# Block-sparse attention and Fourier mixing on one core: another order of the last output products and stores, and the first pair's k load cut in two

## The chip, the cores and the metric

The kernel runs as one program on one core of a Trainium2 chip. The core has a matrix engine (TensorE, "PE" in the profile; its weight loads are listed apart as "PEld"), a vector engine (VectorE, "DVE"), an activation engine (ScalarE, "ACT"), a general engine (GpSimd, "POOL") and a queue engine (SyncE, "SP"). SP and ACT both issue transfers here; the profile calls SP's transfer queue q1 and ACT's q10, and writes "SPq" and "ACTq" for the time in which the two issue them. All transfers run on the core's 16 DMA engines. The metric is the device time of one execution in microseconds (us), the median over several runs.

## The reference

Four batches, eight heads, 768 positions, head width 64. Attention is masked by blocks of 32: a block sees its neighbours, the first and the last block, and three sampled blocks.

```python
scores = scale * np.matmul(q, k.transpose(0, 1, 3, 2))
scores = np.where(mask, scores, -1000000000.0)
attn = softmax(scores)                       # over the last axis
x = np.matmul(attn, v)                       # then (B, H, S, D) -> (B, S, H*D)
u = x + np.real(fft(fft(x, axis=1), axis=2))
un = (u - mean(u)) / sqrt(var(u) + 1e-6)     # over the 512 channels
out = u + np.maximum(un @ w_ch1, 0.0) @ w_ch2    # 512 -> 2048 -> 512
```

## The kernel before, in words

**Attention.** Two heads of one batch make a pair; there are 16 pairs, and a pair goes through 12 units of one score product each (128 keys by 2 x 384 queries). `load_q` and `load_k` fetch a pair's rows, `turn` transposes them on PE and copies them to SBUF, `scores` (L569) multiplies, `weigh` takes the exponential on ACT (L589), `values` multiplies with v (L642). For the first pairs the mask is added by a second, small matmul (L579). A function `slot` runs two units at a time and puts other work between them by estimated times (`when`, `busy`, `gap`); what it plans is fixed when the program is built, and the order of the instructions on each engine is the order in which the code records them.

**The start.** The first pair's loads are recorded first: `load_k(0, nc.scalar)` puts both heads of k on ACT's queue (two transfers, 768 packets of 256 bytes each), `load_q(0)` puts q in six parts on SP's queue (three thirds `t` of the positions times two heads, 256 packets each). ACT then issues v of that pair. SP goes on with a weight chunk (`w_load`), the six parts of the next pair's q, another chunk, the next pair's k, and so on. On PE six matmuls of the unit matrix keep the engine busy (`warm`, L309); then `turn(0, 1, 0)` transposes the first half of k (three of its six chunks of 128 positions), `turn(0, 0, 0)` the first four of six parts of q (that is `t` = 0 and 1), seven more unit matmuls follow, and then come the first scores. The second half of k is transposed after the first two units, and `t` = 2 of q in slot 1. Every transfer counts on one of eight semaphores in turn, so that each one also waits until the transfer eight before it has landed.

**The weights.** w_ch1 and w_ch2 come in chunks of 512 KB and are split into the form that the matmuls want by ACT (L456, L459) and DVE during the first pairs.

**Mixing and channel mixing.** After a batch's attention, `mixer` computes the Fourier sums, the normalised rows, and the two channel products. For the last batch, which has nothing else to run beside it, both products use seven multiplications in place of eight (Winograd's form of Strassen's scheme): `quad` for the first product (seven products of 1.29 us each) and `outputs(r, m, after)` for the second. `outputs` is called for two halves r of the 2048 channels and, in each, for three blocks m of 128 rows; its code names four quarters of such a block's result: `a0` and `a1`, the left and right 256 columns of 128 rows in the first half of the positions (tile xA), and `b0` and `b1`, the same for 128 rows of the second half (xB). Each of its seven products is four matmuls of 128 x 256 into one PSUM buffer: two buffers "m", two "s", one "t" and one "o". `plus` adds a product to its quarter on DVE (L1166). The seven in the order before:

1. a11 with a block of w_ch2 (PSUM "m"): into u by an ACT copy (L1175), and into a0
2. a12 (PSUM "m"): into a0, which is then complete
3. a21 with right sum 2 (PSUM "t"): into u; then u into a1
4. left sum 1 with right sum 1, called `p5` (PSUM "o"): into a1 and, later, into b1
5. left sum 3 with right sum 3 (PSUM "s"): into u; then u into both halves of xB at once (L1188)
6. left sum 4, called `p3` (PSUM "m"): into a1, which is then complete
7. a22 with right sum 4 (PSUM "s"): into b0, which is then complete

Between them `ahead(j)` lets DVE compute the four left sums of the next block of rows (`output_left`, L1142), for m = 0 and 1; the sums 1 to 4 have to be made in that order, since sum 2 is written over a21.

**The stores.** In the second half (r = 1) `store(half, m, cols, queue)` (L1104 to L1107) writes 128 rows of the output. Because of the symmetry that the Fourier part uses, the rows of a block lie in the output in runs that `_ORDER` lists, and `_rows` makes them into transfers: block 0 and block 2 of the first half are two transfers of 64 rows each; block 1 has four, of 1, 63, 63 and 1 rows; in the second half block 3 (m = 0) and block 5 (m = 2) are one transfer of two runs of 64 rows, written "2x64" below, and block 4 (m = 1) is three, of 1, 2x63 and 1 rows. For the very last block of rows (`ends`: r = 1 and no next block) `store(1, m)` is cut by columns: 256 columns (b1) after step 5, and b0 in two parts of 128 columns at the end, one on SP's queue and one on ACT's.

**The exit.** After the last block the code has a branch over a second program (`general`, for inputs with very large scores; L1574). Each engine takes that branch when its own list ends; SP then waits for the eight transfer semaphores, and the engines meet in a last barrier.

Of the kernel before, what the change touches and what calls it, by code (L numbers as in the profile page):

```python
# [22 lines left out]
def _words(ap, n):  # L23

    return bass.DRamTensorHandle(ap.tensor.name, (2 * n,), I32)
# [57 lines left out]
def _rows(view, tile):  # L83

    got = []
    for t, p0, runs, jump, n, s0, step in _ORDER:
        if t != tile:
            continue
        at = view[s0:s0 + 1, :]
        row, col = list(at.ap[0])[0], list(at.ap[1])  # L90
        if jump > 0:
            got.append((p0, runs * n, bass.AP(tensor=at.tensor, offset=at.offset,
                                              ap=[[jump * row, runs], [step * row, n], col])))
            continue
        for r in range(runs):
            at = view[s0 + r * jump:s0 + r * jump + 1, :]
            got.append((p0 + r * n, n, bass.AP(tensor=at.tensor, offset=at.offset,
                                               ap=[[step * row, n], col])))
    return got
# [3 lines left out]
def kernel(  # L103
# [14 lines left out]
    nc = tc.nc  # L118

    B, H, S, D = q.shape  # L120
    DM = H * D
    FF = w_ch1.shape[1]
    P = 128
    C = S // P
# [8 lines left out]
    T = C // 2  # L133
# [48 lines left out]
    ps_s = ctx.enter_context(tc.tile_pool(name="ps_s", bufs=2, space=PSUM))  # L182
    ps_o = ctx.enter_context(tc.tile_pool(name="ps_o", bufs=1, space=PSUM))
# [5 lines left out]
    when = {"PE": 0.0, "ACT": 0.0, "DVE": 0.0, "POOL": 0.0}  # L189
    free = {"m": [0.0, 0.0], "t": [0.0]}  # L190

    def busy(engine, us, after=0.0):
        when[engine] = max(when[engine], after) + us
        return when[engine]
# [23 lines left out]
    def load_blocks(n, a, tile):  # L218


        b, j = pairs[n]
        for i in range(2):
            rows = (q, k)[a][b, 2 * j + i].rearrange("(t r) (g d) -> g r t d", r=BLK, d=BLK)
            for g in range(D // BLK):
                p0 = D * i + BLK * g
                nc.sync.dma_start(
                    out=tile[p0:p0 + BLK, :].rearrange("r (t d) -> r t d", d=BLK), in_=rows[g])
        loaded[n, a] = tile

    def load_k(n, queue=None):  # L230

        if n >= BY_VECTOR:
            load_blocks(n, 1, ld.tile([P, S], FP32, tag="k", name="kb"))
            return
        b, j = pairs[n]
        kt = loaded.get((n, 1))
        if kt is None:
            kt = ld.tile([P, C, 2, D], FP32, tag="k", name="kr")
        for i in range(2):
            (queue or nc.sync).dma_start(out=kt[:, :, i, :],  # L240
                                         in_=k[b, 2 * j + i].rearrange("(p c) d -> p c d", p=P))
        loaded[n, 1] = kt

    def load_q(n):

        if n >= BY_VECTOR:
            load_blocks(n, 0, ld.tile([P, S], FP32, tag="q", name="qb"))
            return
        b, j = pairs[n]
        qt = loaded.get((n, 0))  # L250
        if qt is None:
            qt = loaded[n, 0] = ld.tile([P, T, 2, 2, D], FP32, tag="q", name="qr")
        for t in range(T):
            for i in range(2):
                rows = q[b, 2 * j + i][2 * P * t:2 * P * (t + 1), :]
                nc.sync.dma_start(out=qt[:, t, :, i, :],
                                  in_=rows.rearrange("(p r) d -> p r d", r=2))
# [36 lines left out]
    def bit(n):  # L294
# [4 lines left out]
    nc.gpsimd.dma_start(out=samp_i.rearrange("a b c -> a (b c)"),  # L299
                      in_=bass.AP(tensor=_words(sampled_blocks, NB * NR), offset=0,  # L300
                                  ap=[[0, NB], [1, 2 * NB * NR]]))
    load_k(0, nc.scalar)
    load_q(0)

    def warm(n):

# [171 lines left out]
    by_pe, to_gather = set(), deque()  # L478
    masks = {"by_pe": True}
# [68 lines left out]
    UP = 2 * C  # L548
    UNITS = len(pairs) * UP
    SLOT = 2  # L550
# [59 lines left out]
    def gather(u):  # L610


        n, w = divmod(u, UP)
        half, c = divmod(w, C)
        if c == 0:
            return
        if c == 1:
            acc_of[n, half] = acc_p.tile([P, 2, HS], FP32, tag="acc", name="acc")
        acc, e = acc_of[n, half], e_of[u]
        start = e_of[u - 1] if c == 1 else acc  # L620
        at = max(e_at[u], acc_at.get((n, half), 0.0))
        if u in by_pe and masks["by_pe"] and w < UP - SLOT and max(when["DVE"], at) + 1.0 < max(when["POOL"], at) + 2.9:
            nc.vector.tensor_tensor(out=acc, in0=start, in1=e, op=ALU.add)
            acc_at[n, half] = busy("DVE", 1.0, at) + HOP
        else:

            for i in range(2):
                nc.gpsimd.tensor_add(out=acc[:, i, :], in0=start[:, i, :], in1=e[:, i, :])  # L628
            acc_at[n, half] = busy("POOL", 2.9, at) + HOP
        e_free[u] = acc_at[n, half]  # L630
# [320 lines left out]
    def mixer(b, xA, xB):  # L951
# [24 lines left out]
        t, s = {}, {}  # L976
# [127 lines left out]
        def store(half, m, cols=slice(0, DM), queue=nc.sync):  # L1104
            x = (xA, xB)[half]
            for p0, cnt, rows in _rows(out[b][:, cols], T * half + m):
                queue.dma_start(out=rows, in_=x[p0:p0 + cnt, m, cols])  # L1107
            if m == T - 1:
                finished.add((b, half))
# [5 lines left out]
        o_t, o_s = {}, {}  # L1115
        DH = DM // 2

        def block(r, k, n):
            return w2_sb[:, 8 * r + 4 * k:8 * r + 4 * k + 4, n * DH:n * DH + DH]
# [25 lines left out]
        def outputs(r, m, after):  # L1145

            if m == 0:
                output_left(m, 1)
                output_left(m, 2)
            a11, a12, a21, a22 = (hs[g, i][:, :, m * P:(m + 1) * P]  # L1150
                                  for i in range(2) for g in range(2))
            a0, a1 = xA[:, m, 0:DH], xA[:, m, DH:DM]
            b0, b1 = xB[:, m, 0:DH], xB[:, m, DH:DM]
            rights = {j: [o_t[j, 0], o_t[j, 1]] for j in (1, 2, 3, 4)}

            def product(pool, tag, a, c):
                ps = pool.tile([P, 512], FP32, tag=tag, name="yy")[:, 0:DH]
                for k in range(4):
                    nc.tensor.matmul(ps, a[:, k, :],  # L1159
                                     c[k // 2][:, k % 2, :] if isinstance(c, list) else c[:, k, :],  # L1160
                                     start=(k == 0), stop=(k == 3))
                busy("PE", 1.75)
                return ps

            def plus(to, a, c=None):
                tt(out=to, in0=a, in1=to if c is None else c, op=ALU.add)  # L1166
                busy("DVE", 0.43)

            def ahead(j):
                if after is not None:  # L1170
                    output_left(after, j)

            u = sum_p.tile([P, DH], FP32, tag="oT", name="u")
            p1 = product(ps_m, "m", a11, block(r, 0, 0))
            nc.scalar.copy(out=u, in_=p1)  # L1175
            plus(a0, p1)
            plus(a0, product(ps_m, "m", a12, block(r, 1, 0)))
            if m == 0:
                output_left(m, 3)
                output_left(m, 4)  # L1180
            plus(u, product(ps_t, "t", a21, rights[2]), u)
            plus(a1, u)
            p5 = product(ps_o, "o", o_s[m, 1], rights[1])
            plus(a1, p5)
            ahead(1)
            plus(u, product(ps_s, "s", o_s[m, 3], rights[3]), u)
            both = xB[:, m, :].rearrange("p (n d) -> p n d", n=2)
            tt(out=both, in0=both,  # L1188
               in1=u.rearrange("p (o d) -> p o d", o=1).broadcast_to([P, 2, DH]), op=ALU.add)
            busy("DVE", 0.7)  # L1190
            plus(b1, p5)
            ends = r == 1 and after is None
            if ends:
                store(1, m, slice(DH, DM))
            ahead(2)
            p3 = product(ps_m, "m", o_s[m, 4], block(r, 1, 1))
            plus(a1, p3)
            if r == 1:
                store(0, m)
            ahead(3)  # L1200
            ahead(4)
            plus(b0, product(ps_s, "s", a22, rights[4]))
            if ends:
                store(1, m, slice(0, P))
                store(1, m, slice(P, DH), nc.scalar)
            elif r == 1:
                store(1, m)

        fl = [[("tm"[h == 1 and m != 1], lambda h=h, m=m: un_flip(h, m), 0.6, 0.55, 0.0)
               for m in range(T)]  # L1210
# [6 lines left out]
              for m, us in (((0, 2), RIGHT), ((1,), COMBINE))]  # L1217
        le = [("d", lambda i=i: left(0, i), 0.0, 0.0, COMBINE) for i in (1, 3, 4)]
        after = ([fl[0][0], sp[1][0]] + le +
                 [fl[0][2], sp[1][2], wh[1][0], fl[0][1], sp[1][1], wh[1][2],  # L1220
                  fl[1][0], fl[1][2], wh[1][1]] + ri[0] + [fl[1][1]] + ri[1])
# [391 lines left out]
```

## Time and profile before

| what | value |
|---|---|
| median of 7 runs | 1065.64 us (1064.47 to 1066.08) |
| the profiled execution's own time | 1064.72 us |
| its span, first to last instruction | 1063.0 us |
| PE busy | 1037.4 us, 98% of the span |
| DVE, ACT, POOL busy | 62%, 35%, 22% |
| mean granted TensorE clock | 0.995 |
| PE idle in the last of 40 slices (1036.4 to 1063.0 us) | about half |
| PE waiting for q at the start | 0.4 us, once |

The profiled execution is longer than its span by 1.72 us, which lies outside the first and the last instruction. All times below are from the span's start. "Idle before, releaser" in a row says how long the engine stood still before it and what ended that; a row with "x8" merges eight instructions of one kind. PE's rows are pipelined, so their durations overlap a little; the chain of waits, which cuts them at their starts, is the better clock for PE.

### The profile page before, as it was taken

The numbers are of one execution on the slowest core, as the hardware profiler recorded it, in microseconds if no ns is written. First come the engines' busy times: TensorE is split into PE (matmuls) and PEld (weight loads), VectorE is DVE, ScalarE is ACT, GpSimd is POOL, SyncE is SP. The second block draws the span as 40 slices with busy tenths as digits, with TensorE's granted clock in tenths as the row PEclk, the third lists the DMA queues.
The fourth block names the chain that finished last, engine by engine and source line by source line (L and its number), as shares of the span: only waits on it lengthen the run. The fifth ranks groups of instructions, "written<-read, shape, count | busy, mean of one in ns | idle before, by whom it ended". The sixth has DMA issues, their size and how long they took to land.

```text
span 1063.0 us, 12409 instructions
## 1 busy us (share of the span) xinstructions
PE 1037.4 (98%) x4390; PEld 536.1 (50%) x4390; DVE 654.2 (62%) x1218; ACT 374.5 (35%) x742; POOL 235.7 (22%) x262
## 2 busy tenths in 40 slices
PE   8999999999999999999999999999999999999995
PEld 4433345444455554444444555444445554578584
DVE  5898995667645445664678364765457355574663
ACT  6978755664030112342441302353221211210210
POOL 1000183537000002454553001256420001000000
PEclk9999999999999999999999999999999999999998
DMA  7757422220000002212230001221000001000001
GB/s 209 225 177 226 121 46 45 45 47 15 1 0 1 1 0 48 59 31 52 42 55 1 1 0 30 60 38 28 11 12 5 1 0 34 27 0 1 1 20 43
DMA packets 120741, 46.65 MB, mean 44 GB/s; under 512 B 108114, under 2 KB 113632, under 8 KB 120672
## 3 DMA queue, kind: packets, MB, share of 16 engines
q1 hardware_dynamic: 118654, 44.92, 16.9%
q10 hardware_dynamic: 1986, 0.85, 0.3%
q8 instruction: 36, 0.59, 0.2%
q14 instruction: 33, 0.27, 0.1%
q0 software_dynamic: 32, 0.01, 0.0%
HBM read 37.11 MB, written 6.29 MB: 41 GB/s over the span
## 4 chain that ended last, share of the span: by engine, by line
PE 90%; ACT 3%; DVE 2%; DMA 2%; issue 1%; SPq 0%; POOL 0%; ACTq 0%; DVEq 0%
PE y L1096 23%; PE z L1040 15%; PE s L569 13%; PE o L642 11%; PE yp L1040 7%; PE yy L1159 7%; PE xp L1040 4%; PE zp L850 2%; PE s L579 1%; PE sp L709 1%; DMA out_dram<-x 1%; PE zp L822 1%; PE sp L723 1%; PE utp L965 1%; PE xt L665 1%
## 5 line engine op out<-in xcount | busy, mean ns | idle before, releaser
L628 POOL TENSOR_TENSOR acc<-acc,e 128x384 f32<-128x384 f32 x158 | 159.4, 1044 | 94.0 <-DVE e L599 75.0
L569 PE MATMUL s<-qT,kT 64*128 64x384 f32 x768 | 153.6, 515 | 7.5 <-ACT e L589 4.0
L642 PE MATMUL o<-e,vr 128*64 128x384 f32 x768 | 142.3, 498 | 0.0
L1096 PE MATMUL y<-w_sb,hB 128*128 128x512 f32 x288 | 128.2, 596 | 1.0 <-DVE x L1099 1.0
L1096 PE MATMUL y<-w_sb,hA 128*128 128x512 f32 x288 | 128.4, 595 | 0.0
L599 DVE TENSOR_TENSOR e<-s,mask 128x768 f32<-128x768 f32 x92 | 83.8, 950 | 57.8 <-ACT s L597 48.0
L1099 DVE TENSOR_TENSOR x<-y,x 128x512 f32<-128x512 f32 x72 | 49.7, 690 | 110.9 <-PE y L1096 110.8
L569 PEld LDWEIGHTS s<-qT,kT 64*128 64x128 f32 x768 | 63.9, 185 | 85.6 <-issue 21.9
L597 ACT ACTIVATE s<-s 128x768 f32<-128x768 f32 x92 | 69.9, 792 | 87.5 <-PE s L569 87.0
L1040 PE MATMUL z<-unT,t 128*128 128x384 f32 x256 | 93.1, 486 | 1.2 <-DVE hA L1045 1.2
L628 POOL TENSOR_TENSOR acc<-e 128x384 f32<-128x384 f32 x42 | 47.1, 1143 | 212.6 <-ACT e L589 127.6
L1045 DVE TENSOR_TENSOR hA<-z,hA 128x384 f32<-128x384 f32 x64 | 35.7, 557 | 87.3 <-PE z L1040 87.3
L589 ACT ACTIVATE e<-s 128x768 f32<-128x768 f32 x100 | 76.2, 816 | 36.7 <-PE s L579 31.6
L1096 PEld LDWEIGHTS y<-w_sb,hB 128*128 128x128 f32 x288 | 53.4, 190 | 67.7 <-issue 64.8
L913 POOL TENSOR_SCALAR st<-st 128x1 f32<-128x1 f32 x24 | 8.6, 359 | 346.9 <-DVE st L912 346.8
L1096 PEld LDWEIGHTS y<-w_sb,hA 128*128 128x128 f32 x288 | 53.3, 190 | 62.8 <-issue 59.7
L642 PEld LDWEIGHTS o<-e,vr 128*64 128x64 f32 x768 | 48.1, 137 | 70.6 <-issue 68.2
L1049 ACT ACTIVATE hA<-hA 128x384 f32<-128x384 f32 x64 | 33.5, 523 | 120.3 <-DVE hA L1045 119.8
L1040 PEld LDWEIGHTS z<-unT,t 128*128 128x128 f32 x256 | 48.5, 190 | 35.5 <-DVE hA L1045 2.1
L1049 ACT ACTIVATE hB<-hB 128x384 f32<-128x384 f32 x64 | 33.5, 523 | 86.5 <-DVE hB L1045 84.1
L1060 ACT COPY hA<-xp 128x384 f32<-128x384 f32 x32 | 15.3, 479 | 97.9 <-PE xp L1040 97.9
L1040 PE MATMUL xp<-unT,w_sb 128*128 128x384 f32 x128 | 47.3, 492 | 0.0
(202 smaller groups left out, 1431.3 us busy)
## 6 DMA issues: line engine op xcount, KB each, us to landing
wraw<-in_moe_w_ch_dram SPq DMA_DIRECT2D x32, 512.0 KB
vr<-in_v_dram SPq DMA_DIRECT2D x30, 192.0 KB
qb<-in_q_dram SPq DMA_DIRECT2D x44, 96.0 KB
kb<-in_k_dram SPq DMA_DIRECT2D x44, 96.0 KB
x<-oT SPq DMA_DIRECT2D x192, 12.0 KB
out_dram<-x SPq DMA_DIRECT2D x17, 128.0 KB
out_dram<-x SPq DMA_DIRECT2D x7, 256.0 KB
qr<-in_q_dram SPq DMA_DIRECT2D x24, 64.0 KB
```

Of the source, the lines that this page charges most:

```text
L569: nc.tensor.matmul(s[:, i, 0:HS], kT[rows, c * P:(c + 1) * P], qT[rows, queries], start=True, stop=u not in by_pe)
L589: nc.scalar.activation(out=e, in_=s[:, :, 0:HS], func=ACT.Exp, scale=scale)
L597: nc.scalar.activation(out=s[:, :, 0:HS], in_=s[:, :, 0:HS], func=ACT.Exp, scale=scale)
L599: nc.vector.tensor_tensor(out=e, in0=s[:, :, 0:HS], in1=m.broadcast_to([P, 2, HS]), op=ALU.mult)
L628: nc.gpsimd.tensor_add(out=acc[:, i, :], in0=start[:, i, :], in1=e[:, i, :])
L642: nc.tensor.matmul(o[D * i:D * i + D, :], vt[:, i, c, :], e[:, i, :], start=(c == 0), stop=(c == C - 1))
L1040: nc.tensor.matmul(to, a[:, k, :], c[:, k, :], start=(k == 0), stop=(k == ND // 2 - 1))
L1045: tt(out=to, in0=ps, in1=a, op=ALU.add)
L1049: nc.scalar.activation(out=h, in_=h, func=ACT.Relu)
L1096: nc.tensor.matmul(y, hs[0, half][:, l, m * P:(m + 1) * P], w2_sb[:, 4 * r + l, :], start=(l == 0), stop=(l == 3))
L1099: nc.vector.tensor_tensor(out=x[:, m, :], in0=y, in1=x[:, m, :], op=ALU.add)
L1159: nc.tensor.matmul(ps, a[:, k, :], c[k // 2][:, k % 2, :] if isinstance(c, list) else c[:, k, :], start=(k == 0), stop=(k == 3))
```

## The change

It has two parts.

**The first pair's loads.** `load_k` takes a list of cuts over the chunks and `load_q` a list of thirds. ACT's queue now gets only the first three of k's six chunks (two transfers of 384 packets); SP's queue gets the thirds 0 and 1 of q (four transfers), then the other three chunks of k (two transfers), then third 2 of q (two transfers). SP issues eight transfers there in place of six.

**The last outputs.** In `outputs`, for both r, product 7 of the list above (a22, into b0) moves to the fourth place, p5 from the fourth place to the sixth, and p3 becomes the last. The sum of p5 into b1 now stands ahead of its sum into a1. `ahead(1)`, `ahead(2)` and `ahead(3)` all come after these, ahead of p3's sum into a1; `ahead(4)` comes after it. With r = 1, block m of xB is stored before block m of xA. For the last block of rows, a0 is stored as soon as it is complete (two transfers of 64 rows x 256 columns on SP's queue), b0 after the sum of step 5 (2x64 rows x 256 columns, one transfer on ACT's queue), b1 after p5 (the same size on SP's queue), and a1 at the very end (two transfers of 64 rows x 256 columns on SP's queue). The condition `sooner` in `gather` is only given a name.

```diff
-    def load_k(n, queue=None):
+    def load_k(n, queue=None, cuts=(slice(0, C),)):
...
-        for i in range(2):
-            (queue or nc.sync).dma_start(out=kt[:, :, i, :],
-                                         in_=k[b, 2 * j + i].rearrange("(p c) d -> p c d", p=P))
         loaded[n, 1] = kt
-
-    def load_q(n):
+        for cs in cuts:
+            for i in range(2):
+                (queue or nc.sync).dma_start(
+                    out=kt[:, cs, i, :],
+                    in_=k[b, 2 * j + i].rearrange("(p c) d -> p c d", p=P)[:, cs, :])
+
+    def load_q(n, ts=range(T)):
...
-        for t in range(T):
+        for t in ts:
...
-    load_k(0, nc.scalar)
-    load_q(0)
+    load_k(0, nc.scalar, (slice(0, T),))
+    load_q(0, range(2))
+    load_k(0, None, (slice(T, C),))
+    load_q(0, range(2, T))
...
+            ends = r == 1 and after is None
             u = sum_p.tile([P, DH], FP32, tag="oT", name="u")
             p1 = product(ps_m, "m", a11, block(r, 0, 0))
             nc.scalar.copy(out=u, in_=p1)
             plus(a0, p1)
             plus(a0, product(ps_m, "m", a12, block(r, 1, 0)))
+            if ends:
+                store(0, m, slice(0, DH))
             if m == 0:
                 output_left(m, 3)
                 output_left(m, 4)
             plus(u, product(ps_t, "t", a21, rights[2]), u)
             plus(a1, u)
-            p5 = product(ps_o, "o", o_s[m, 1], rights[1])
-            plus(a1, p5)
-            ahead(1)
+            plus(b0, product(ps_s, "s", a22, rights[4]))
             plus(u, product(ps_s, "s", o_s[m, 3], rights[3]), u)
             both = xB[:, m, :].rearrange("p (n d) -> p n d", n=2)
             tt(out=both, in0=both,
                in1=u.rearrange("p (o d) -> p o d", o=1).broadcast_to([P, 2, DH]), op=ALU.add)
             busy("DVE", 0.7)
+            if ends:
+                store(1, m, slice(0, DH), nc.scalar)
+            p5 = product(ps_o, "o", o_s[m, 1], rights[1])
             plus(b1, p5)
-            ends = r == 1 and after is None
-            if ends:
-                store(1, m, slice(DH, DM))
+            if r == 1:
+                store(1, m, slice(DH if ends else 0, DM))
+            plus(a1, p5)
+            ahead(1)
             ahead(2)
+            ahead(3)
             p3 = product(ps_m, "m", o_s[m, 4], block(r, 1, 1))
             plus(a1, p3)
             if r == 1:
-                store(0, m)
-            ahead(3)
+                store(0, m, slice(DH if ends else 0, DM))
             ahead(4)
-            plus(b0, product(ps_s, "s", a22, rights[4]))
-            if ends:
-                store(1, m, slice(0, P))
-                store(1, m, slice(P, DH), nc.scalar)
-            elif r == 1:
-                store(1, m)
```

More of the change, by code (lines that the diff above doesn't have):

```diff
@@ L621, in gather @@
         at = max(e_at[u], acc_at.get((n, half), 0.0))
-        if u in by_pe and masks["by_pe"] and w < UP - SLOT and max(when["DVE"], at) + 1.0 < max(when["POOL"], at) + 2.9:
+        sooner = max(when["DVE"], at) + 1.0 < max(when["POOL"], at) + 2.9
+        if u in by_pe and masks["by_pe"] and w < UP - SLOT and sooner:
             nc.vector.tensor_tensor(out=acc, in0=start, in1=e, op=ALU.add)
```

## The prediction

> **What bounds the kernel now.** I read the page first: its span, PE's row and the busy share in 40 slices.
>
> ```profile
> span 1063.0 us, 12409 instructions
> ...
> PE 1037.4 (98%) x4390; PEld 536.1 (50%) x4390; DVE 654.2 (62%) x1218; ACT 374.5 (35%) x742; POOL 235.7 (22%) x262
> ...
> PE   8999999999999999999999999999999999999995
> ```
>
> PE is busy for 98% of the span, and what it lacks lies in the first slice and the last. Neither part of the change takes a matmul away. So only the two ends can give time, and I read each from its chain of waits. First the start (columns: start, duration, what):
>
> ```profile
> 3.14 3.94 DMA qr<-in_q_dram
> 7.08 0.14 issue
> 7.21 0.41 PE tp L502 x2
> 7.63 1.56 PE warm L309 x14
> 9.19 1.49 PE s L569 x8
> ```
>
> The fourth part of q is issued at 3.14 and lands at 7.08. PE's row for the transposes ahead of it starts at 6.13 and lasts 0.64, so PE is free at 6.77 and stands for 0.45 us, the one wait for q in the list of waits. Everything after hangs on PE in order. Now the end, from the chain, the timeline and the instructions of the exit branch (L1574):
>
> ```profile
> 1015.54 36.27 PE yy L1159 x168
> 1051.81 0.02 issue
> 1051.83 0.42 DVE x L1166
> ```
>
> ```profile
> 1052.29 0.55 SPq L1107 DMA_DIRECT2D out_dram<-x  x1
> 1052.29 1.38 ACTq L1107 DMA_DIRECT2D out_dram<-x  x1
> ```
>
> ```profile
> L1574 DVEq COMPARE_BRANCH x1: 72/72/72, 1051.8 to 1051.8; - x1
> L1574 SPq COMPARE_BRANCH x1: 50/50/50, 1052.9 to 1052.9; - x1
> L1574 ACTq COMPARE_BRANCH x1: 62/62/62, 1053.7 to 1053.7; - x1
> L1574 DVEq EVENT_SEMAPHORE x1: 21/21/21, 1056.4 to 1056.4; - x1
> L1574 ACTq EVENT_SEMAPHORE x1: 17/17/17, 1061.4 to 1061.4; - x1
> ...
> SPq L1574 <- SPq L1574: 8.1, 1, 8.1
> ```
>
> The 21 products of the last half run without a gap, 1.727 us each, to 1051.81. DVE adds the last one by 1052.25, and at 1052.29 two stores are issued. SP branches at 1052.9 and then waits 8.1 us, to 1061.0; from there to the span's end are 2.0 us of barrier. So 8.7 us lie between the last store's issue and SP's release, against 0.4 us on DVE. What fills them is seen in the transfers, taken in windows of time. The lines below are, in order: 1028 to 1029 (block 0, transfers of 64 rows), 1030 to 1033 and 1046 to 1048 (2x64 and 2x63 rows of 2 KB), 1051 to 1052.5 (b1 alone, 2x64 rows of 1 KB), 1057 to 1058 (two lines) and 1058 to 1060 (two lines). Columns: packets, MB, share of 16 engines.
>
> ```profile
> q1 hardware_dynamic: 118, 0.21, 89.9%
> ...
> q1 hardware_dynamic: 48, 0.10, 12.1%
> ...
> q1 hardware_dynamic: 50, 0.10, 13.1%
> ...
> q1 hardware_dynamic: 49, 0.05, 11.6%
> ...
> q1 hardware_dynamic: 79, 0.04, 13.3%
> q10 hardware_dynamic: 6, 0.00, 1.0%
> ...
> q10 hardware_dynamic: 120, 0.06, 10.1%
> q1 hardware_dynamic: 23, 0.01, 1.8%
> ```
>
> A transfer of 64 rows keeps nearly all 16 engines busy. A transfer of two runs keeps 12 to 13% of 16 busy, which is two engines, whatever the rows' size. And when SP's and ACT's 128-column parts of b0 run together, the sum is no more than that (13.3 + 1.0%): they share the two. The four last packets come between 1060.0 and 1060.5. So the end is bound by two slow engines, on which b1, shares of a0 and a1, and both parts of b0 queue up one after the other; PE is long done.
>
> **The last outputs, part by part.** *Same work on PE:* 21 products of 1.727 us, so PE ends at 1051.81 as before. *Order of products:* every operand of the new order is ready: right sum 4 and left sum 3 of block m = 0 end at 1017.34 and 1020.12 in the trace, and are first needed at the fourth and fifth product, 1020.72 and 1022.45. Cost nothing, hidden under the products ahead. *Later left sums:* a wait is added here. p3's buffer "m" is needed again by the second product of the next block. Take the change of block at 1039.72: p5 ends at 1037.99; behind it DVE has two sums at 0.34 to 0.46 (pairs of rows 0.34 and 0.46 apart), left sums 1 and 2 at 0.72 (the sum behind each needs the one before: 1017.25 to 1017.97), sum 3 at 0.60, and p3's sum, 0.42. That ends at 1041.2; the second product's matmul would start at 1041.45 and its weight load 0.22 us earlier. So the wait is 0 to 0.1 us, four times (two per half): 0 to 0.4, I take 0.15. What queues behind it on PE is the whole remaining row of products; on DVE the left sum 4 and the sums into a0, which nothing needs for another 3 us.
>
> *Stores.* SP's queue in order: for m = 0 and 1 the transfers are the same with halves swapped. Block 4 (2x63 rows) is issued at about 1038.7 and not 1040.7, so its packets, which last until 1048.3 now, end by 1046.3, or by 1048 with shares of block 1's transfers between them. Its semaphore is the one that b0's store on ACT waits for, at 1049.57: cover 1.5 us. a0 (two transfers, two issues of 0.55 us each) is complete at 1043.6, and goes out in the shadow of block 4. b0 is complete when L1188 ends (1048.84 + 0.69 = 1049.53) and is issued on ACT, which has nothing else. b1 is issued at about 1050.56, after p5 (1050.08) and its sum. a1 is complete at 1052.25 as b0 was; its two issues last to 1053.4, 0.55 more than now.
>
> On the two engines lie then, from 1050.6 (issue plus 1.0 us, as with b1: issued 1050.02, first packets at 1051.1): 128 packets of b0, 128 of b1, and a1's share, 2 engines x 4 packets x 2 = 16; 272 of 1 KB. What the two do per us with 1 KB is not seen alone for long. From below: b1's first 1.5 us, 49 packets, 33 per us. From above: 79 per us with 512 bytes (1057 to 1058) and 25 with 2 KB (1046 to 1048) are 12.7 and 40 ns per packet; a straight line between gives 21.8 ns, 46 per us. So 5.9 to 8.2 us; I take the slow rate for the first half (it is each transfer's beginning) and the fast one for the rest: 130/33 + 142/46 = 7.0, to 1057.6. From the last packets (1060.2) to SP's release (1061.0) it took 0.8: 1058.4, bounds 1057.3 and 1059.6. Now it is 1061.0: **-2.6 us** (-3.7 to -1.4).
>
> This needs SP to be past its branch by then. DVE's first instruction after its branch came 4.6 us later. SP's branch moves to 1053.45, so 1058.05 by that row, just covered by the transfers. ACT took 7.7 us; by that row SP would run only at 1061.2, and the gain would be gone (rival 1). SP's own time is hidden in its 8.1 us of waiting. ACT's branch itself moves ahead by 2.7 us.
>
> The Trainium skill speaks against the full gain here: in "Runtime: NRT & Kernel Launch", section "Instruction fetch mechanics", it says that a taken branch whose target isn't in the current window forces a DMA fetch of the target page before execution can continue. It has no price; with DVE's row as the price of that fetch the sum stays at -2.6, with ACT's row it falls to zero.
>
> **The first loads.** All 16 engines are busy while q's first parts come: 1046 packets between 4 and 5 us, 423 of them k's. Of k's 1536 packets half go behind q's fourth part: at some 1000 per us that part could land 0.77 earlier, of which PE can use 0.45. Against it stands v on ACT's queue: its first transfer waits now for a part of q (issued 3.99) and then for a part of k, so it can come 0.3 earlier and push in front of q. Bounds -0.45 and +0.3; I take **-0.35**, near the first, because 768 packets go away and 256 come 0.3 us sooner. Moved behind: k's second half at the fifth and sixth place of SP's queue (issued about 3.8 and 4.45); with the 3.94 of the q part it lands by 8.4, and PE transposes it at 10.94. q's third 2 waits for two semaphores and is issued by 6.4, lands by 10.4, needed at 16.63. The weight chunk comes two issues (1.3 us) later; it had landed by 10.37, when the transfer that waits for its semaphore was issued, and ACT needs it at 18.67. Cover 8 us. Later loads wait for room, not for the queue. The gain then rides through the stall at 64.9 to 70.8 (ACT waits 3.0 us for a chunk), whose loads are released by DVE and so come earlier too.
>
> **Sum.** -2.6 - 0.35 + 0.15 = -2.8 on the profiled execution: 1064.72 becomes 1061.9. The median of the runs is 0.92 above that execution, so 1065.64 becomes **1062.8 us**.
>
> **Rivals.**
>
> 1. *The exit waits for its instructions, not for the stores.* For it: ACT needed 7.7 us from branch to next instruction. Against it: DVE needed 4.6, and ACT's was perhaps held up by the same two engines. Then SP runs at 1061.2, +0.2, and the sum is -0.35 + 0.15 + 0.2: about 1065.6, no change.
> 2. *The two big halves of xB choke the two engines* (the one that ends slower). b0 is now one transfer of 128 KB beside b1 in place of two of 64 KB behind it, and a1's shares queue last. In 1030 to 1033 the two engines did only 48 packets in 3 us, 16 per us, with 2 KB. If packets of 1 KB from two queues go no faster, 272 take 17 us, to 1067.6, released at 1068.4: +7.4, about 1072.8. It decides from a release at 1063.3 on, which is 22 packets per us. Against it: 33 per us in b1's own first part.
> 3. *The halves don't share engines.* Then b1 and its share of a1 (136 packets) end by 1055.7, SP is released by 1056.5 if its instructions are there: tail -4.5, about 1060.9. Against it: the sum of 13.3 and 1.0%.
> 4. *The start does nothing*, because v takes the room that k leaves: 1063.1, inside the forecast's own range.
>
> **How the numbers follow.** The forecast (with rival 4 in it) gets 66%; its own range is 1061.6 to 1063.9 from the bounds of the tail. About 0.2% (2.1 us) is what a measurement of this kernel can tell from no change: 1063.5. Four fifths of the forecast lie below that (53 points), one fifth within (13). Rival 1 gets 16%, all of it "same"; rival 2 gets 7%, "slower"; rival 3 gets 11%, "faster". Faster 0.64, same 0.29, slower 0.07. The range goes from 1061.0, which leaves some 7 points of rival 3 out, to 1065.8, which takes in rival 1 and leaves rival 2 out.
>
> **What would show it.** After: SP's release comes at about 1058, two-run packets run to about 1057.6 at 12 to 13% with both queues among them, PE's last product ends near 1051.6, and PE's wait for q is gone. Right for the blocks: PE's second product of a block waits for DVE by 0.1 us at most. The forecast is wrong if SP's first instruction after the branch comes with no transfer landing just before it (rival 1), or if the two-run packets go on past 1060 (rival 2).

## The result and the profile after

The changed kernel takes 1061.66 us (median of 14 runs, 1061.14 to 1062.81) against 1064.76 us for the kernel before (34 runs, 1063.42 to 1067.39). The ratio is 0.9971, 95% interval 0.9964 to 0.9978: 3.1 us less (2.3 to 3.8). The forecast was 1062.8, made against a median of 1065.64. The first lines of the page, span, PE's row and PE's busy share in 40 slices:

```profile
span 1060.1 us, 12422 instructions
...
PE 1037.0 (98%) x4390; PEld 535.9 (51%) x4390; DVE 654.7 (62%) x1218; ACT 374.3 (35%) x742; POOL 235.6 (22%) x262
...
PE   8999999999999999999999999999999999999996
```

PE does what it did (1037.4 us before) in a span that is 2.9 us shorter; only the last slice looks different. The end of the chain of waits of the changed kernel:

```profile
1014.77 36.37 PE yy L1164 x168
1051.13 0.02 issue
1051.16 0.42 DVE x L1171
```

The last half's products begin at 1014.77 (1015.54 before), take 36.37 us (36.27), and PE ends at 1051.13 (1051.81). The exit branch of the changed kernel is L1580. Its rows give an engine's branch and its first instruction behind it (columns: duration in ns, then first and last start); the last line is SP's wait there, in total, times, longest:

```profile
L1580 SPq EVENT_SEMAPHORE  x8: 17/17/17, 1056.3 to 1058.4; - x8
...
L1580 ACTq COMPARE_BRANCH  x1: 58/58/58, 1050.0 to 1050.0; - x1
...
L1580 DVEq COMPARE_BRANCH  x1: 72/72/72, 1051.2 to 1051.2; - x1
L1580 SPq COMPARE_BRANCH  x1: 50/50/50, 1052.8 to 1052.8; - x1
L1580 DVEq EVENT_SEMAPHORE  x1: 21/21/21, 1054.0 to 1054.0; - x1
L1580 ACTq EVENT_SEMAPHORE  x1: 17/17/17, 1055.5 to 1055.5; - x1
...
SPq L1580 <- SPq L1580: 5.3, 4, 3.5
```

SP's first instruction comes 3.5 us behind its branch, at 1056.3. (This time, from an engine's branch to its next instruction, is called the fetch below, where no transfer holds the instruction up.) Three more waits follow, the last of them, for the second part of a1, to 1058.23: 7.10 us behind PE's last product, where it was 9.16 (1051.81 to 1060.97). The queues of the changed kernel's transfers, first from 1050 to 1053.9, then from 1055 to 1056.6 (columns: packets, MB, share of 16 engines; q8 and q14 carry instructions):

```profile
q10 hardware_dynamic: 128, 0.13, 12.0%
q1 hardware_dynamic: 15, 0.02, 3.4%
q8 instruction: 1, 0.02, 1.5%
q14 instruction: 1, 0.01, 0.5%
...
q1 hardware_dynamic: 76, 0.08, 13.4%
```

ACT's b0 (q10) has two engines almost to itself: its 128 packets of 1 KB run from 1050.18 to 1053.96, 3.8 us, and two packets of four bytes, one for each of the two engines, signal its end. SP's b1 was issued at 1049.88, and all 15 packets of SP's queue in that window come in its last 0.5 us. Then q1 has the two engines, at 48 packets per us. So the two stores share the pair, as the forecast had it, but one behind the other and not mixed: the first of the two engines signals its end of b0 at 1053.62 and starts on b1 there, the other goes on with b0 to 1053.96.

### The profile page after: what moved, and what is told of

Same layout as the page of the kernel before. It is cut to its first block, busy times and chain, and to the rows that moved or that the text cites. A ratio compares the mean times of both kernels' runs of the same rounds, so it can differ in the third digit from the quotient of the medians.

```text
span 1060.1 us, 12422 instructions
## 1 busy us (share of the span) xinstructions
PE 1037.0 (98%) x4390; PEld 535.9 (51%) x4390; DVE 654.7 (62%) x1218; ACT 374.3 (35%) x742; POOL 235.6 (22%) x262
## 4 chain that ended last, share of the span: by engine, by line
PE 89%; DVE 3%; DMA 3%; ACT 2%; issue 1%; SPq 0%; POOL 0%; ACTq 0%; DVEq 0%
PE y L1101 23%; PE z L1045 15%; PE s L573 12%; PE o L647 11%; PE yp L1045 7%; PE yy L1164 7%; PE xp L1045 4%; PE zp L855 2%; DMA out_dram<-x 1%; PE s L583 1%; PE sp L714 1%; PE zp L827 1%; PE sp L728 1%; PE utp L970 1%; PE xt L670 1%
```

## The experiments

Every time below stands against runs of the kernel before on the same chip, taken in the same set. "Tail" is the time from the end of PE's last product to the last wait behind the branch that anything held up. Differences in us are worked out from the ratio, which can differ by some tenths of a us from the difference of the two medians.

**The loads alone**: the kernel before with the new `load_k`, `load_q` and this.

```
-    load_k(0, nc.scalar)
-    load_q(0)
+    load_k(0, nc.scalar, (slice(0, T),))
+    load_q(0, range(2))
+    load_k(0, None, (slice(T, C),))
+    load_q(0, range(2, T))
```

> The kernel before with only the new order of the first loads; outputs as before. The theory (the loads gave the 0.77 us by which PE's last half begins earlier, 1014.77 against 1015.54): 0.6 to 0.9 us below the kernel before, the second unit's transposes (PE tp of k's second half) at about 9.9 instead of 10.94, and about 0.74 of that left after the wait for a weight chunk at 64 to 71 us. SP's release stays about 9.1 us behind PE's last product. Rival (the earlier PE comes from the outputs' order or from chance): no difference.

Measured: 1064.10 against 1064.83, ratio 0.9996 (0.9987 to 1.0005): 0.4 us less, with an interval from 1.4 less to 0.5 more. (The two medians are 0.7 apart. The interval holds that, and it holds no change.) In its profile the first scores begin at 9.11, as late as before (9.12). The expectation missed: it had taken the 0.77 us of a single pair of profiles for the effect of the loads.

**The outputs alone**: the kernel before with the changed `outputs`.

> The kernel before with only the new outputs; loads as before. The theory: 2.0 to 2.3 us below the kernel before (tail 9.16 to about 7.1, barrier 0.17 shorter, block waits 0.10 longer), so that this and the loads alone add up to the whole change, 2.9. Rival (the two parts need each other): less than 1.5 or more than 2.8.

Measured: 1062.88 against 1064.83, ratio 0.9978 (0.9969 to 0.9987), 2.3 us less (1.4 to 3.3). Tail 7.13 (1053.06 to 1060.19). The outputs make most of the gain, and they need nothing from the loads. This is as expected.

**The changed kernel with b0 and b1 as one run.** The last block's rows of xB go to every second row, descending, in two runs of 64. Here the same rows are written in ascending order, as one run of 128, so they hold each other's values: a probe, not a kernel to use.

```
+            if last and half and m == T - 1:
+                first = out[b][386:387, cols]
+                to = [(0, P, bass.AP(tensor=first.tensor, offset=first.offset,
+                                     ap=[[2 * DM, P], list(first.ap[1])]))]
...
```

> The changed kernel with the last block's b0 and b1 stored as one run of 128 rows in place of two runs of 64: the same 128 rows of the output, but in ascending order, so these rows hold each other's values. Same bytes, same number of instructions and queues. Two engines bind the end (theory): the two stores spread over 16 engines, the last transfer to land is a1's at 1055 to 1056, and SP's release falls from 1058.2 to 1056.3 or 1056.5, where SP's first instruction after its branch (3.5 us) takes over as the bound: 1.6 to 2.0 us below the changed kernel, 4.5 to 5.0 below the kernel before. Rival 1 (the exit waits for instructions already, or for the receipt of writes): no more than 0.3 below the changed kernel.

Measured: 1059.90, ratio 0.9954 (0.9940 to 0.9967), 4.9 us less; tail 4.63. The queues from 1049.7 to 1050.3, and then from 1050.7 to 1051.4:

```profile
q10 hardware_dynamic: 144, 0.13, 62.5%
q14 instruction: 1, 0.01, 6.2%
...
q1 hardware_dynamic: 144, 0.13, 53.5%
```

The same 128 KB that took 3.8 us on two engines take 0.5 us (b0 from 1049.77 to 1050.25, b1 from 1050.76 to 1051.31), with 16 packets of four bytes that signal the end, where b0 in two runs had two. And b1 comes 1.0 us behind b0 and not 3.4. All has landed by 1054.7, but SP's first instruction comes only at 1055.78, 2.6 us behind its branch: the fetch binds now, as expected. One number was off: SP's branch came at 1053.21 and not at 1052.8, because the second issue of a1 took 1.02 us, and the fetch was faster than the 3.5 us that I had taken; the two cancel.

**The kernel before with its last xB stores as one run**: the same edit, in the kernel before.

> The kernel before with the last block's b1 and both parts of b0 stored as one run of 128 rows each (same rows of the output, ascending, values of the rows exchanged); order of products and loads as before. Two engines bind the end (theory): the stores land 2 to 3 us after their issue at 1052.29, so SP is released when its instructions are there, at 1056.4 by its own 3.5 us; or, if ACT's branch (1053.7) takes 5.5 us again, ACT comes last at 1059.2. So 1.8 to 4.6 us below the kernel before, with nothing moved; the order of products and the split into halves are then not what counts. Rival (the order of products is what gave the gain): no difference.

Measured: 1058.77, ratio 0.9945 (0.9931 to 0.9958), 6.1 us less; tail 3.8. This is more than the 1.8 to 4.6 expected, since SP's fetch took 2.9 us and not the 3.5 reckoned with, and ACT's 2.9 and not 5.5. It is also faster than the changed kernel with the same edit. The branch rows show why:

```profile
L1580 SPq EVENT_SEMAPHORE  x8: 17/17/17, 1055.0 to 1055.6; - x8
...
L1580 SPq COMPARE_BRANCH  x1: 50/50/50, 1052.1 to 1052.1; - x1
L1580 ACTq COMPARE_BRANCH  x1: 62/62/62, 1052.1 to 1052.1; - x1
...
L1580 ACTq EVENT_SEMAPHORE  x1: 17/17/17, 1055.1 to 1055.1; - x1
```

Behind the last product SP and ACT have one issue each, of 0.36 and 0.38 us, where the changed kernel has SP issue twice. SP branches 0.9 us behind PE's end and not 2.1 as in the paragraph before, and ACT's fetch takes 2.9 us, not 7.7 as in the kernel before. So the old order was good, but for its two-run transfers. On these runs the new order is worth something only because it takes these out of the last microseconds.

**b0 and b1 one product earlier** (a12's product in the last block goes behind p5).

```
-            plus(a0, product(ps_m, "m", a12, block(r, 1, 0)))
-            if ends:
-                store(0, m, slice(0, DH))
+            if not ends:
+                plus(a0, product(ps_m, "m", a12, block(r, 1, 0)))
...
             plus(a1, p5)
+            if ends:
+                plus(a0, product(ps_m, "m", a12, block(r, 1, 0)))
+                store(0, m, slice(0, DH))
```

> The changed kernel, and in the last block the product of a12 goes behind p5, next to last; so b0 and b1, the two stores that lie on two engines, are complete one product (1.73 us) earlier, and a0's store (64-row transfers) goes out at about 1050 in place of 1045. Nothing else moves. Two engines bind the end (theory): b0 and b1 end at 1055 to 1055.5, the shares of a0 and a1 (32 packets) behind them, release at 1056.4 to 1056.8 in place of 1058.2: 1.4 to 1.8 us below the changed kernel, 4.5 to 4.9 below the kernel before. Rival (fetch of SP's instructions behind the branch has become the bound at 1056.3 or later than that): 1.9 at most. Rival (what counts is the time from the last store to its receipt): no difference from the changed kernel.

Measured: 1060.86 against 1065.22, ratio 0.9963 (0.9949 to 0.9977), 1.2 below the changed kernel in the same set; tail 5.99, against 7.10 and 6.91 in the two profiles of the changed kernel. Right in direction and cause, 0.2 short in size: the shares of a0 and a1 on the two engines were the last to land, at 1057.44.

**The same, with a1's second store on ACT.** Edit: `store(0, m, ...)` alternates between SP's and ACT's queue in the last block.

> As the kernel with a12's product behind p5, and the second of a1's two last stores goes on ACT's queue in place of SP's. SP branches at about 1052.2 in place of 1052.8, ACT too. If transfers bind at 1056.4 to 1056.8: the same time as with both on SP's queue, within 0.2. If the fetch behind SP's branch (2.6 to 3.5 us) binds: 0.5 less, 4.9 to 5.4 below the kernel before. If ACT's fetch takes the 5.5 us again that it took in the changed kernel: release at 1057.7, 0.9 to 1.3 more.

Measured: 1060.07, ratio 0.9958 (0.9944 to 0.9972); tail 5.75. SP was through at 1056.86, 4.7 us behind PE's end, but ACT branched at 1053.16 and came back at 1057.88. The slow fetch of ACT is the bound here. None of the three cases of the expectation came as it stood: ACT's fetch took 4.7 us and not 5.5, so the time is not 0.9 to 1.3 longer than with both stores on SP's queue. By the two intervals no difference between these two kernels can be told.

**The changed kernel and the kernel before once more.**

> The changed kernel itself, beside the other two on one chip, and as a second profile of its start. If the start's gain is real and steady, PE's first scores begin at about 8.1 again; if the moment at which q's parts land varies from run to run, anywhere between 8.1 and 8.6. Time: 2.3 to 3.8 us below the kernel before.

> The kernel before, for a second profile of its start. With the same loads the first scores began at 9.12 in the kernel before; in the two kernels of the first set that keep these loads the copies of qT that they wait for came 0.43 and 1.03 earlier. If that is chance: anywhere between 8.1 and 9.1. If it hangs on the kernel's code: 9.1 again.

Measured: 1062.06 for the changed kernel (ratio 0.9971, 0.9961 to 0.9982), tail 6.91; 1064.50 for the single run of the kernel before, tail 9.73. What they show of the start needs three timelines (columns: start, duration, what). The kernel before, first profile:

```profile
7.47 1.73 PE L309 MATMUL warm<-ident 128*128 128x128 f32 x14
9.12 1.56 PE L569 MATMUL s<-qT,kT 64*128 64x384 f32 x8
```

The kernel before, second profile:

```profile
6.34 1.73 PE L309 MATMUL warm<-ident 128*128 128x128 f32 x14
8.00 1.56 PE L569 MATMUL s<-qT,kT 64*128 64x384 f32 x8
```

And the kernel of the paragraph before this one, with the new loads:

```profile
6.80 2.65 PE L313 MATMUL warm<-ident 128*128 128x128 f32 x14
9.38 0.92 PE L573 MATMUL s<-qT,kT 64*128 64x384 f32 x4
```

The same loads gave 9.12 and then 8.00. In the four profiles with the old loads the first scores begin at 9.12, 8.00, 9.29 and 8.09, in the nine with the new loads (leaving out the kernel with fewer fillers) between 8.12 and 9.38: means 8.63 and 8.68. PE's wait for q (0.45 us) stands in the first profile of the kernel before and in no other of the fourteen. What does differ is the rate of PE: the 14 fillers take 1.73 us in some runs and up to 2.65 in others, since they follow each other at 0.21 us first and at 0.11 later, and the moment of the change differs from run to run.

**b0's store issued by POOL** (`nc.scalar` becomes `nc.gpsimd` in that store), with a12's product behind p5; and **the same with a1's second store on ACT.**

> As the kernel with a12's product behind p5 (1060.86; from PE's last product to SP's last wait 5.99 us), with b0's store issued by POOL in place of ACT. Where b0 and b1 queue on one pair of engines because both are the lowest-numbered two, a transfer that POOL issues may come to lie on another pair. Then b1's packets begin about 1 us after b1's issue and not behind b0's, all has landed by about 2.9 us behind SP's branch, and SP's fetch (2.6 to 3.5 us) sets the release: 4.2 to 5.0 us behind PE's last product, 1.0 to 1.8 below that kernel, 5.4 to 6.2 below the kernel before. Rival (POOL's transfer lies on the same pair): the same time, within 0.3, b1 behind b0 again.

> As the last, and the second of a1's last stores on ACT's queue: SP and ACT both branch about 1.0 us behind PE's last product. If ACT's first instructions come late (5.5 us in the changed kernel, 4.7 with a12's product behind p5 and this split) because a transfer of two runs lies on the two engines meanwhile, they come 2.7 to 3.0 us behind the branch now, and the last wait ends 3.7 to 4.2 us behind PE's last product: 6.0 to 6.6 below the kernel before. Rival (ACT's fetch takes 4.7 or more whatever the stores do): 5.7 us behind PE's last product, 4.4 to 5.0 below the kernel before.

Measured: 1060.43 (ratio 0.9958, 0.9945 to 0.9971), tail 5.74; and 1061.72 (0.9972, 0.9960 to 0.9983), tail 6.68. Both expectations missed. With POOL's issue the queues from 1050 to 1052.5 are these:

```profile
q0 software_dynamic: 94, 0.08, 12.1%
q1 hardware_dynamic: 30, 0.03, 8.9%
```

b1 is no longer behind b0, its packets begin at 1050.1, but only 30 packets of SP's queue start in 2.5 us (12 per us) while POOL's transfer runs. In both kernels SP's queue still had packets behind 1055.5 (to 1056.3 and 1056.6). In the second one ACT's fetch took 5.4 us again (to 1057.47), and SP's half of a1 landed only at 1057.63. Whether POOL's transfer lay on the same pair, or slowed b1 in another way, these runs don't settle.

**Three fillers in place of seven** ahead of the first scores.

```
-    warm(7)
+    warm(3)
```

> The changed kernel with 3 in place of 7 filler products (6 in place of 14 matmuls) between q's transposes and the first scores; they compute nothing that is used. In ten profiles so far, with either order of loads, the first scores began between 8.00 and 9.38, and late where the fillers run at the slow rate (2.65 us for 14 against 1.73). If PE's rate and the fillers set the start: the scores begin at 8.1 to 8.5 whatever the moment of the change of rate, the moment itself stays, and the time falls by 0 to 0.9, 0.4 in the mean, against the changed kernel. Rival (q's transposes and ACT's copies set it): the scores begin as before, at 8.1 to 9.4.

Measured: 1061.21 against 1064.56, ratio 0.9966 (0.9954 to 0.9979); against the changed kernel's 0.9971 no difference can be told. The scores begin at 7.29, earlier than in any other profile and than either case of the expectation had it, and they wait 0.22 us for ACT's copy of qT, so the fillers did hold them. But PE's last half begins at 1014.73, as in the changed kernel (1014.77). Of the 0.83 us by which the scores begin earlier, nothing is left there; ACT's wait for a weight chunk between 60 and 100 us has grown by more. First the changed kernel, then this one (columns: total, times, longest):

```profile
ACT wraw L460 <- DMA wraw<-in_moe_w_ch_dram: 3.5, 2, 3.3
```

```profile
ACT wraw L460 <- DMA wraw<-in_moe_w_ch_dram: 4.8, 2, 4.0
```

**b0 and b1 well ahead of the end.** The two last products of the block before, with its a stores, go behind the last block's p5, as does the last block's own product of a12, and a1's second store goes on ACT's queue. The left sums of the last block move up to where they are needed.

```
+            holds = r == 1 and m == T - 2
...
+            if holds:
+                ahead(3)
+                ahead(4)
+
+                def rest():
+                    plus(a0, product(ps_m, "m", a12, block(r, 1, 0)))
+                    plus(a1, product(ps_m, "m", o_s[m, 4], block(r, 1, 1)))
+                    store(0, m)
+
+                held.append(rest)
+                return
+            if ends:
+                held.pop()()
...
```

> The changed kernel with three things: in the last block a12's product goes behind p5; the two last products of the block before (a12's and p3's, with the store of its a0 and a1) go behind the last block's p5 as well, so that b0 and b1, the transfers of two runs, are complete 3.5 us earlier still and gone from the two engines before PE ends; and the second of a1's two last stores goes on ACT's queue. If two engines bind the end and also hold up the fetch of instructions behind a branch (5.4 to 7.7 us for ACT in every profile with such a transfer under way, 2.7 and 2.9 in the two profiles without), SP and ACT branch about 1.0 us behind PE's last product and come 2.6 to 3.0 us later: 3.6 to 4.2 us from PE's last product to the last wait, 5.2 to 5.9 below the kernel before. Rival (ACT's fetch takes 4.7 or more whatever lies on the two engines): 5.7 or more from PE's last product, 3.4 to 4.6 below the kernel before.

Measured: 1059.72 against 1065.00, ratio 0.9950 (0.9936 to 0.9964): 5.3 us below the kernel before, and the lowest time here of a kernel that writes the right output, though its interval overlaps those of the two nearest (0.9958 both). Its branch rows:

```profile
L1599 SPq EVENT_SEMAPHORE  x8: 17/17/17, 1055.7 to 1056.2; - x8
...
L1599 SPq COMPARE_BRANCH  x1: 50/50/50, 1052.3 to 1052.3; - x1
L1599 ACTq COMPARE_BRANCH  x1: 58/58/58, 1052.4 to 1052.4; - x1
...
L1599 ACTq EVENT_SEMAPHORE  x1: 17/17/17, 1056.0 to 1056.0; - x1
```

The last transfer lands at 1055.30, and ACT's first instruction at 1056.02 ends the tail, 4.69 us behind PE's end, where 3.6 to 4.2 had been expected. The fetches took 3.4 (SP) and 3.7 us (ACT), 0.4 to 0.7 more than expected; but ACT's is a full microsecond below the fastest with a two-run transfer under way.

## Why the prediction was right, and where it was not

**The tail (-2.6) was the right term with the right cause.** On the two profiles that were compared it is -2.06 (9.16 to 7.10). Over all profiles with either set of outputs and the stores as they were, the tail is 9.16, 9.73 and 9.36 before (mean 9.42) and 7.10, 6.91, 7.13 and 7.11 after (mean 7.06): -2.4. The one-run experiments show the cause: the same bytes spread wide took the queueing away in both orders. (They also turn the order of the rows round, which was not tested by itself. That the number of engines changed is seen from the packets.) The Trainium skill has the rule behind it, in "DMA: Bandwidth & Descriptors", section "Why a DMA increments its semaphore by 16 and not by 1": a transfer goes to as many engines as the largest number up to 16 that divides the slowest dimension of both of its patterns, and a queue of SP or ACT always takes the lowest-numbered ones. The traces agree on the number: two packets that signal the end and 12.0% of 16 engines for two runs of 64, sixteen and 62.5% in a window of 0.6 us for one run of 128. Which engines they are the traces don't show, but that SP's and ACT's stores queue on one pair fits.

**Two details of the tail were wrong.** I had b0 and b1 share the two engines from 1050.6 on; they ran one after the other. This didn't change the sum, since 272 packets are 272 packets. The rates, 33 per us for the first half and 46 for the rest, came out as 34 for b0 (128 in 3.8 us) and 48 at the end. And b0's first packet came 1.29 us behind its issue (1048.89 to 1050.18), where the forecast had 1.0 from b1's row (1050.02 to 1051.1; by the packets it was 1051.19, 1.17). The last packet of a1 came at 1057.42, 7.24 us behind b0's first and not 7.0. These two make up the 0.5 by which the tail of this pair fell short.

**The first loads (-0.35) failed as a step, though its size can't be refuted.** The step read "PE is free at 6.77 and stands for 0.45 us" as a property of the kernel. It was one of that execution: three later profiles with the same loads have no such wait. Comparing only the two profiles would have made it worse, by crediting the loads with 0.77. The runs give -0.4 with an interval from -1.4 to +0.5, and the mean start of the first scores is the same with both. So rival 4, that the start does nothing, is not excluded. PE's last half begins at 1015.47 in the mean of the four profiles with the old loads (1014.66 to 1016.70) and at 1015.01 in that of the nine with the new ones (1014.65 to 1015.81): 0.46 earlier, which is less than the four differ among themselves. The forecast had the gain ride through the stall at the weight chunk. In part it does: in the six profiles with 14 fillers whose scores begin by 8.43 (mean 8.18) the last half begins at 1014.78, in the seven others (9.08) at 1015.48, so 0.7 of 0.9 us arrives. But of the further 0.83 us of the kernel with fewer fillers nothing did.

**The blocks (+0.15) came out as +0.10**: 36.37 against 36.27 us, and PE's list of waits for the last half has this line.

```profile
PEld yy L1164 <- DVE x L1171: 0.4, 2, 0.2
```

**The rivals.** Rival 1, an exit bound by its instructions, is a real mechanism, at a price of 3.5 us for SP and not ACT's 7.7; in the changed kernel SP was back 1.9 us before its last wait ended, so it cost nothing. It became the bound as soon as the transfers were out of the way (one run, and b well ahead). The skill's "Runtime: NRT & Kernel Launch", section "Instruction fetch mechanics", which says that a branch out of the window has to fetch its target by DMA, fits the rows of instruction packets on q8 and q14; it has no price, and here the time was not the same with and without two-run transfers. For ACT it was 4.7 to 8.2 us in the eleven profiles with a two-run transfer under way, and 2.7, 2.9 and 3.7 us in the three others. The packets show the link itself. In each of the eleven an instruction packet of 8 KB starts 1.5 to 1.7 us ahead of ACT's first instruction. In the five in which b0 is ACT's last transfer it starts within 0.01 us of b0's end (1053.96 in the changed kernel). In the kernel before it stands in the midst of b0's part: q10 and q14 from 1059.55 to 1059.8, from 1059.8 to 1060.1 and from 1060.1 to 1060.2.

```profile
q10 hardware_dynamic: 11, 0.01, 7.4%
...
q14 instruction: 1, 0.01, 6.4%
...
q10 hardware_dynamic: 4, 0.00, 5.6%
```

The store stands still for just the 0.31 us that the instruction packet takes, and then goes on. So ACT's fetch ran on one of the two engines that its own store was queued on, as the forecast had guessed against rival 1. Rival 2, a choke below 22 packets per us, did not come: b0's first 70 packets took 2.3 us, 30 per us, and its slowest us (1051.5 to 1052.5) had 26. Rival 3, that the halves share nothing, fell with the windows of the changed kernel.

**The sum.** -2.8 was forecast and -2.9 found on the two profiled executions, but the agreement is better than its terms: -0.77 at the start, +0.10 in the blocks, -2.06 in the tail and -0.15 in the barrier behind it. The tail gained 0.5 less there than forecast, and the start 0.4 more, by chance: two misses that cancel. The medians (-3.1, interval -3.8 to -2.3) hold the forecast as well.

## What to carry to other kernels

Before reordering the last work of a kernel, look at how many engines its last stores use and at what each queue still has to issue behind the last result: here the shape of two stores cost more than the whole change gained. An engine that leaves by a branch can pay for its own slow store a second time, in its fetch, as ACT did. A wait that stands in one profile is a sample; take the start from two or three executions before a term is built on it. And an early gain must be followed to the next stall, which may keep a part of it or all.

## What the hardware showed that I had not expected

- PE's rate in the first microseconds differs between executions of one kernel: 14 fillers take 1.73 to 2.65 us, and the first scores move by up to 1.4 us with it. The granted clock in the profile's windows stands at 1.00 all the while. But the record of the clock in the traces starts only with the change: its first entry, of 1.00, lies at 5.87 in the second profile of the kernel before, at 8.72 in the slowest, and between 5.66 and 8.72 in the fourteen. The skill's "TensorE: Matmul & The Clock Gate", section "Part 1: The HAM clock gate (the "warmup" mystery)", says that the gate looks at a free-running window of some 3.4 us, so that the moment varies from run to run. That the moment varies agrees with these profiles: PE's first work begins at 2.6 in all of them, and its fast rate (fillers 0.11 us apart in place of 0.21) at those moments, 3.1 to 6.1 us later. But the page gives the spread as half a us to either side, and here it is 3.1 us in all.
- The instructions behind the exit branch came 2.6 to 3.6 us later for SP where no transfer held it, 2.9 to 4.5 for DVE, 2.7 to 8.2 for ACT, and only 0.6 for POOL in the quiet middle of the kernel (891.2 to 891.8). In the two kernels in which POOL issued b0 and branched at 1047.7 and 1047.6 it was 0.2.
- Two-run transfers from SP's and ACT's queue ran one behind the other on each of the two engines (in the changed kernel b1's first packet starts within 0.01 us of the first engine's last of b0, at 1053.62), while POOL's ran beside SP's, of which only 12 packets per us started meanwhile. ACT's b0 began at about 30 packets per us in each profile and reached 48 after 2 to 2.5 us; SP's b1 behind it ran at 48 at once. Why is open.
